# A transformer block on one core: the second visit's second stage starts two products later, and VectorE makes the low halves of both 64-row operands

## Chip, cores and metric

The kernel runs on one core of one Trainium2 chip. The metric is the device time of one execution in microseconds; the time before is a median of 3 runs.

## What is computed

One block with adaptive layer normalisation over 2048 tokens of width 576, all in fp32: attention with 32 query heads of width 18 and one shared key and value head, then an MLP of width 4608.

```python
mod = (_silu(c) @ w_mod).reshape(c.shape[0], 6, 1, -1)
sa, ca, ga, sb, cb, gb = (mod[:, i] for i in range(6))
h = _layernorm(x) * (1 + ca) + sa
x = x + ga * attention(h, wq, wk, wv, wo)
h = _layernorm(x) * (1 + cb) + sb
y = _layernorm(h)                       # the MLP normalises once more
h = _gelu(y @ w1 + b1)                  # 576 -> 4608, tanh form
x = x + gb * (h @ w2 + b2)              # 4608 -> 576
```

## The kernel before

Only the MLP, the last part of the kernel, is touched. It works on two halves of 1024 tokens. For each half it walks over 18 groups of 256 hidden columns, so there are 36 visits, `v` = 0 to 35; visit 17 is the last of the first half and visit 18 the first of the second. The loop over `v` starts at line 1208.

Each matrix product of a visit is done by a Strassen-like scheme with seven products instead of eight. In the first stage these are A11, S2, S3, A12, S1, A22 and S4, issued in that order by `product` (line 1042). To keep fp32 accuracy every operand is split into a high half, rounded to the matmul's type (a ScalarE copy), and a low half, the rest (a subtraction). Each product is 6 matmuls: high by high, high by low and low by high for two blocks of 128 rows. The width 576 is four blocks of 128 rows and one of 64. The 64-row rest is held in the tile `opt` (`TL[0]` in the code) as the operands t0 and t1, high and low half each; A12 and A22 read t0, and S1 and S4 read t1, with two further matmuls each.

`op_pieces` (line 956) holds the table of these operands: name, first block in the destination, first block in the source, and the engine that does the low-half subtraction. The function it returns, `form`, reads strings such as "+t0 -t0": plus is the high half (ScalarE, line 974), minus is the low half (line 976), and "=T1" is a sum of blocks (line 967). The engine `e2` is VectorE for what is formed before the loop and GpSimd afterwards. The operands of the second half of the tokens are formed in pieces by `more` during visits 17 and 18: "-t0" at the end of visit 17, "-t1" after product S2 of visit 18. GpSimd does there also the sum for T1, and the low halves of B21, T4 and B22.

After the first stage come the GELUs (`gelu`, line 1056), on ScalarE and VectorE. A GELU is cut into three parts; each call of `g_()` moves every open one forward by a part. The sums of GELU outputs that the second stage needs are made by GpSimd (`sums`, line 1116): `s_()` does the next of four, first S3's, then S2's, S1's and S4's. Each is one or two additions, a cast to the high half (line 1123) and a subtraction for the low half (line 1124).

The second stage of visit v (`fc2s`, line 1138) is interleaved with the first stage of visit v + 1. It is a generator with seven steps, for S3, A22, A11, A12, S2, S1 and S4, called by `t_()`. A step issues 12 matmuls into two `psA` tiles, two evictions by VectorE that add them to the residual (line 1156; line 1154 where a sum is begun), and the load of the step's weights for the next visit on the SyncE queue. S3, A11, S2 and S1 begin new `psA` tiles. There are two of these, so a step that begins new ones waits for the evictions of the step before; the other steps add to what is in the tiles, and their matmuls wait for those evictions too. In a usual visit the order on TensorE is A11, step 7 of the visit before the last, S2, step 1, S3, step 2, A12, step 3, S1, step 4, A22, step 5, S4, step 6. In visit 1 there is no seventh step of an earlier visit, so the first step comes behind A11 and S2. The four `psB` tiles hold the results of the products.

The SyncE queue also carries, behind each product, the load of that product's weights for the next visit (`w_`, line 1232). The layer normalisation of the second half of the tokens (`ln2_pair`) runs in visits 1 to 17, a piece in each call of `more`. The order of instructions on each engine is the order written in the program.

Of the kernel before, what the change touches and what calls it, by code (L numbers as in the profile page):

```python
# [32 lines left out]
def block_kernel(ctx: ExitStack, tc, x, wqkv, wo, w1, b1, w2, b2, c, wmod, ident_in, out):  # L33
    nc = tc.nc
    ve, ac, po, pe, sy = nc.vector, nc.scalar, nc.gpsimd, nc.tensor, nc.sync
# [17 lines left out]
    def psB(): return PS["t"].tile([128, 512], F32, name="psB", bufs=PS["b"])  # L53
# [650 lines left out]
    def load_w1(i, what):  # L704
        for w in what.split():
            a = 4 * OPS.index(w) if w in OPS else 28
            b = min(a + 4, 31)
            sy.dma_start(W1["r"][:, a:b].bitcast(F32), w1scr[i, :, a:b])
# [117 lines left out]
    def step(q):  # L826
        if q:
            try:
                next(q[0])
            except StopIteration:  # L830
                q.popleft()
# [124 lines left out]
    def op_pieces(R, e2):  # L956


        at = {"B11": (0, 0, ve), "B21": (2, 2, e2), "B22": (4, 7, e2), "T2": (6, 5, ve), "T1": (8, 5, ve),
              "T3": (10, 0, ve), "T4": (12, 2, e2), "t0": (0, 4, e2), "t1": (1, 9, e2)}  # L960
        less = {"T3": (5, 0, 0), "T4": (2, 5, 2), "T1": (7, 5, 5)}

        def form(what):
            for w in what.split():
                if w[0] == "=":
                    x, y, o = (R[:, i:i + 2] for i in less[w[1:]])
                    (e2 if w == "=T1" else ve).tensor_tensor(o, x, y, op=ALU.subtract)
                    continue
                a, r, e = at[w[1:]]
                n = 2 if w[1] in "BT" else 1  # L970
                o, lo = (OP, 14) if n == 2 else (TL[0], 2)
                hi, src = o[:, a:a + n], R[:, r:r + n]
                if w[0] == "+":
                    ac.activation(hi, src, AF.Copy)
                else:
                    e.tensor_tensor(o[:, lo + a:lo + a + n], src, hi.bitcast(F32), op=ALU.subtract)
        return form

    form = op_pieces(YR[0], ve)
    open_ps("3", 4)  # L980
    wop = {}

    def wo_tile(t, k0, k1):
        if t not in wop:
            p = psA() if t != 2 else None
            wop[t] = [psB()[:, :288] if t == 2 else p[:, h2, :288] for h2 in range(2)], p
        for h2 in range(2):
            wo_mm(NB - 1, t, h2, wop[t][0][h2], k0, k1)
        if k1 == KD:
            o, p = wop[t]  # L990
            if p is None:
                for h2 in range(2):
                    wo_add(NB - 1, t, h2, o[h2])
            else:
                Xv = XT[:, NT * (NB - 1) + t, :].rearrange("p (a b) -> p a b", a=2)
                ve.tensor_tensor(Xv, p[:, :, :288], Xv, op=ALU.add)
# [25 lines left out]
    def wo_end():  # L1022

        pwp.__exit__(None, None, None)
        mw = ctx.enter_context(tc.tile_pool(name="mw", bufs=1, reuse_waits="tile"))
        a = [mw.tile([128, 2, D], F32R, name="w2s", bufs=3) for _ in range(3)]
        a.append(W1["r"][:, 31:40].rearrange("p a b -> p (a b)").rearrange("p (f c) -> p f c", f=2))
        W2.extend(a[:2])
        W2S.extend(t.rearrange("p f (n c) -> p (f n) c", c=288)[:, i:i + 2] for t in a for i in (0, 2))
        GT.append(big())  # L1030
        g2 = mw.tile([128, 4, TB], F32R, name="gt2")
        GT.extend([g2[:, i] for i in range(4)] + [mw.tile([128, TB], F32R, name="gt3"), W1["r"][:, 36:40].rearrange("p a b -> p (a b)")])
        for k in range(7):
            load_w2s(0, k)
# [7 lines left out]
    def product(o, w, b, first=True, tail=None):  # L1042

        w = 4 * OPS.index(w)
        h, l = W1["r"][:, w:w + 2], W1["r"][:, w + 2:w + 4]
        terms = []
        for k in range(2):
            terms += [(h[:, k], OP[:, b + k]), (h[:, k], OP[:, 14 + b + k]), (l[:, k], OP[:, b + k])]
        if tail:
            wt = W1["r"][:, 28 + tail[0]]  # L1050
            terms += [(wt, TL[0][:, tail[1]]), (wt, TL[0][:, 2 + tail[1]])]
        for i, (x, y) in enumerate(terms):
            pe.matmul(o, x, y, start=(first and i == 0), stop=(i == len(terms) - 1), skip_group_check=True)  # L1053
# [46 lines left out]
    def pair_end():  # L1100
        v = NG - 1
        for to in ((1, 0), (1, 1), (0, 1)):
            eb_add(v, *to)
            yield
        for t in range(2 * NT):
            sy.dma_start(out[128 * t:128 * (t + 1), :], XT[:, t, :])
            yield
# [84 lines left out]
    def t_():  # L1192
        step(f2)

    def s_():
        step(sm)

    def g_():

        for gen in list(gens):  # L1200
            if next(gen, 0) == 0:
                gens.remove(gen)

    form = op_pieces(YR[0], po)
    b2_scaled(B2["b"])
    mark = [None]

    for v in range(NV):
        nxt = (v + 1) % NG
        if v == NG - 1:  # L1210
            while fill:
                step(fill)
            form = op_pieces(YR[1], po)

        def more(half="", first="", room=False):

            if v in (0, NG - 1, NG):
                form(first if v == 0 else half if v == NG - 1 else {"+T4": "-T4 +T1 -B22", "-T4": "-T1 -t1"}.get(first, ""))
            elif v > NG + 1 and fill:
                step(fill)  # L1220
            elif 0 < v < NG and fill and (room or mark[0] != "T"):
                mark[0] = next(fill[0], "end")
                if mark[0] == "end":
                    fill.popleft()
            if v == 0 and rest:
                for _ in range(2):
                    if rest:
                        wo_tile(*rest.popleft())
                if not rest:
                    wo_end()  # L1230

        def w_(w):
            if v + 1 < NV:
                load_w1(nxt, w)

        if v == NG + 1:
            fill.append(pair_end())
        ba = psB()
        product(ba, "A11", 0)
        w_("A11")  # L1240
        ac.activation(U[:, 0], ba, AF.Copy)
        g_()
        s_()
        more("+B11", "+T4")
        if v > 1:
            t_()
        bb = psB()
        product(bb, "S2", 6)
        w_("S2")
        ve.tensor_tensor(U[:, 0], bb, U[:, 0], op=ALU.add)  # L1250
        t_()
        g_()
        more("-B11 +T2", "-T4")
        bc = psB()
        product(bc, "S3", 10)
        w_("S3")
        ve.tensor_tensor(U[:, 1], bc, U[:, 0], op=ALU.add)
        s_()
        more("-T2 =T3", "+B22", True)
        t_()  # L1260
        product(ba, "A12", 2, False, (0, 0))
        w_("A12")
        gens.append(gelu(v, 0, 0, ba))
        g_()
        s_()
        more("+T3 +B21", "-B22", True)
        t_()
        g_()
        bd = psB()
        product(bd, "S1", 8, True, (1, 1))  # L1270
        w_("S1")
        be = psB()
        ve.tensor_tensor(be, bd, U[:, 1], op=ALU.add)
        g_()
        gens.append(gelu(v, 1, 1, be))
        g_()
        more("-T3 -B21")
        t_()
        g_()
        product(bc, "A22", 12, False, (1, 0))  # L1280
        w_("A22")
        ve.tensor_tensor(bc, bc, U[:, 0], op=ALU.add)
        g_()
        gens.append(gelu(v, 1, 0, bc))
        g_()
        more("=T4 +t0")
        t_()
        g_()
        product(bd, "S4", 4, False, (2, 1))
        w_("S4 tails")  # L1290
        ve.tensor_tensor(bd, bd, U[:, 0], op=ALU.add)
        g_()
        gens.append(gelu(v, 0, 1, bd))
        g_()
        t_()
        more("=T1 +T4 -t0 +B22 +t1")
        if v == NV - 1:
            while f2:
                t_()
        if v < NV - 1:  # L1300
            sm.append(sums(v))
            s_()
            f2.append(fc2s(v))
        else:
            f2.append(fc2(v))
# [44 lines left out]
```

## Time and profile before

| | |
|---|---|
| median of 3 runs | 2281.99 us (2280.32 to 2283.0) |
| the profiled execution | 2280.29 us, span 2278.5 us |
| TensorE matmul, share of the span busy | 98% (16534 instructions) |
| VectorE, ScalarE, GpSimd | 85%, 72%, 66% |
| matmuls of the first stage, blocks of 128 rows (line 1053) | 1512, 395.7 us busy |
| matmuls of the second stage with operands in the tile `big` (line 1150) | 1680, 248.3 us busy |

Times inside the execution count from the start of the span. The MLP's loop fills it from about 1410 us on. Rows of the form "line engine operation output<-input" give the line of the kernel, and the part in brackets at the end of a timeline row is how long the engine sat idle before it and which instruction ended that wait. PEld is the load of TensorE's stationary operand, which runs ahead of the matmul that uses it.

### The profile page before, as it was taken

How to read it: one execution, taken by the hardware profiler on the slowest of the kernel's cores; microseconds unless marked ns; L12 is line 12 of the kernel's file. 1: busy time of each engine (PE TensorE's matmuls, PEld its weight loads, DVE VectorE, ACT ScalarE, POOL GpSimd, SP SyncE). 2: the span in 40 equal slices, each digit the busy share in tenths (PEclk: the TensorE clock that was granted, in tenths of full speed). 3: DMA queues.
4: the chain of work that ended last, by engine and by line, in shares of the span. 5: the costliest groups of instructions: out<-in, count | busy, mean ns of one | idle time of the engine just before them, and what ended most of it. 6: DMA issues, size and time to landing. Idle time of an engine off the chain costs nothing.

```text
span 2278.5 us, 45948 instructions
## 1 busy us (share of the span) xinstructions
PE 2241.0 (98%) x16534; PEld 1446.2 (63%) x16534; DVE 1942.0 (85%) x3435; ACT 1644.9 (72%) x3141; POOL 1506.1 (66%) x1759
## 2 busy tenths in 40 slices
PE   8999999999999999999999999999999999999999
PEld 6644545444444444444444546888888878888888
DVE  6589999999999999999999974778888777787786
ACT  5558999999999999999999997444454444343443
POOL 6503366676787787677783002888888887767676
PEclk9999999999999999999999999999999999999999
DMA  6421234433433333333331002555656557666563
GB/s 225 138 99 49 73 124 142 136 128 117 135 124 121 119 132 114 119 125 123 119 129 64 20 7 83 180 174 178 177 173 180 160 151 215 180 178 179 177 181 117
DMA packets 184229, 305.58 MB, mean 134 GB/s; under 512 B 19275, under 2 KB 77515, under 8 KB 184001
## 3 DMA queue, kind: packets, MB, share of 16 engines
q1 hardware_dynamic: 184001, 302.64, 42.1%
q8 instruction: 131, 2.15, 0.4%
q14 instruction: 97, 0.79, 0.1%
HBM read 200.48 MB, written 93.19 MB: 129 GB/s over the span
## 4 chain that ended last, share of the span: by engine, by line
PE 90%; DVE 5%; POOL 2%; ACT 2%; issue 1%; DMA 0%; ACTq 0%; POOLq 0%; DVEq 0%
PE psC L845 22%; PE psB L1053 17%; PE psA L1150 16%; PE psB L855 14%; PE psM L315 11%; PE psB L657 2%; PE psB L244 2%; DVE mx L877 2%; PE psB L865 2%; PE psB L152 1%; ACT P L857 1%; PE psA L315 1%; PE psB L199 1%; PE psA L1180 1%; PE psA L657 1%
## 5 line engine op out<-in xcount | busy, mean ns | idle before, releaser
L857 ACT ACTIVATE P<-psB 128x512 f32<-128x512 f32 x2008 | 1044.8, 619 | 45.3 <-PE psM L315 18.4
L877 DVE TENSOR_REDUCE mx<-psM 128x1 f32<-128x512 f32 x1476 | 938.1, 683 | 42.4 <-PE psB L855 19.6
L315 PE MATMUL psM<-KS,qst 64*128 64x512 f32 x1722 | 600.1, 440 | 1.1 <-DVE mx L877 0.4
L855 PE MATMUL psB<-qst,KS 64*128 64x512 f32 x2008 | 584.5, 428 | 0.6 <-DVE mx L333 0.4
L845 PE MATMUL psC<-P,V 128*32 128x256 f32 (+3 forms) x6424 | 578.8, 448 | 0.5 <-ACT O L672 0.5
L855 PEld LDWEIGHTS psB<-qst,KS 64*128 64x128 f32 x2008 | 302.2, 184 | 215.6 <-ACT P L857 132.8
L1053 PE MATMUL psB<-ops,w1a 128*128 128x512 f32 x1512 | 395.7, 397 | 0.2 <-DVE h L1068 0.2
L315 PEld LDWEIGHTS psM<-KS,qst 64*128 64x128 f32 x1722 | 274.5, 184 | 157.2 <-DVE mx L877 122.4
L1053 PEld LDWEIGHTS psB<-ops,w1a 128*128 128x128 f32 x1512 | 271.4, 189 | 45.9 <-DVE h L1068 0.4
L1156 DVE TENSOR_TENSOR XT<-psA,XT 128x576 f32<-128x576 f32 x350 | 256.4, 753 | 18.5 <-PE psA L1150 11.5
L845 PEld LDWEIGHTS psC<-P,V 128*32 128x32 f32 x6424 | 139.4, 108 | 202.9 <-issue 176.7
L1150 PE MATMUL psA<-w2s,big 128*128 128x288 f32 x1680 | 248.3, 297 | 6.4 <-POOL big L1123 2.6
L1150 PEld LDWEIGHTS psA<-w2s,big 128*128 128x128 f32 x1680 | 240.0, 190 | 21.7 <-POOL big L1123 3.5
L1124 POOL TENSOR_TENSOR big<-s,big 128x512 fp32r<-128x512 f32 x140 | 181.9, 1299 | 11.2
L1066 ACT ACTIVATE psB<-gs 128x512 f32<-128x512 f32 x144 | 86.7, 602 | 135.5 <-DVE gs L1065 135.5
L1062 ACT ACTIVATE h<-psB,b1t 128x512 f32<-128x512 f32 x144 | 98.0, 680 | 109.1 <-PE psB L1053 93.7
L875 DVE CUSTOM_DVE_ANT_0 xc<-psM,xc 128x512 f32<-128x512 f32 x246 | 166.0, 681 | 3.7 <-PE psB L855 1.2
L868 ACT ACTIVATE xc<-psB 128x512 f32<-128x512 f32 x246 | 152.9, 622 | 11.9 <-PE psM L315 11.9
L691 POOL TENSOR_TENSOR os<-O,os 128x512 fp32r<-128x512 f32 x28 | 36.1, 1290 | 150.5 <-ACT os L690 150.5
L1065 DVE SCALAR_TENSOR_TENSOR gs<-psB,h 128x512 f32<-128x512 f32 x144 | 98.5, 684 | 39.3 <-ACT psB L1063 39.3
L718 POOL TENSOR_TENSOR r<-r,r 128x256 fp32r<-128x256 f32 (+1 forms) x162 | 121.4, 749 | 13.0
L132 POOL MEMSET qst<- 32x1024 f32 x62 | 58.6, 945 | 106.8 <-PE psB L855 69.0
(198 smaller groups left out, 3238.9 us busy)
## 6 DMA issues: line engine op xcount, KB each, us to landing
w1a<-w1scr SPq DMA_DIRECT2D x252, 256.0 KB
w2s<-w2sum SPq DMA_DIRECT2D x140, 288.0 KB
w1scr<-r SPq DMA_DIRECT2D x126, 256.0 KB
w2scr<-r SPq DMA_DIRECT2D x72, 288.0 KB
w2sum<-r SPq DMA_DIRECT2D x72, 288.0 KB
w2s<-w2scr SPq DMA_DIRECT2D x70, 288.0 KB
qst<-qscr SPq DMA_DIRECT2D x192, 72.0 KB
w1a<-w2scr SPq DMA_DIRECT2D x35, 288.0 KB
```

Of the source, the lines that this page charges most:

```text
L315: pe.matmul(o, QST[n][64 * g:64 * g + 64, p, 128 * qt:128 * (qt + 1)], KS[64 * g:64 * g + 64, 512 * kb:512 * (kb + 1)], start=True, stop=True)
L718: po.tensor_tensor(o[:, n:2 * n], src, o[:, :n].bitcast(F32), op=ALU.subtract)
L845: pe.matmul(PVt[n][32 * j:32 * (j + 1), cs], V[:, kc, :], t[:, j, cs], start=(kc == 0 and h0 == 0), stop=(kc == 15), skip_group_check=True)
L855: pe.matmul(t, KS[64 * g:64 * g + 64, 128 * kc:128 * (kc + 1)], QST[n][64 * g:64 * g + 64, i, :], start=True, stop=True)
L857: ac.activation(P[n, kc][:, 2 * i + g, :], t, AF.Exp, scale=SCALE)
L868: ac.activation(XC[-1], t, AF.Relu)
L875: ve.tensor_tensor_reduce(c, t, c, 1.0, -3.0e38, ALU.add, ALU.max, o)
L877: ve.tensor_reduce(o, t, axis=AX.X, op=ALU.max)
L1053: pe.matmul(o, x, y, start=(first and i == 0), stop=(i == len(terms) - 1), skip_group_check=True)
L1124: po.tensor_tensor(unit(u, 1), x, unit(u, 0).bitcast(F32), op=ALU.subtract)
L1150: pe.matmul(p[:, i, :288], x[:, ts_], W2S[k][:, y], start=(bool(first) and q == 0), stop=(q == 2), skip_group_check=True)
L1156: ve.tensor_tensor(o, p[:, :, :288], o, op=ALU.add)
```

## The change

In visit 1, and only there, the calls of `t_()` after products S2 and S3 are left out, and a second call is added after S1 and after A22. The order on TensorE in visit 1 becomes A11, S2, S3, A12, step 1, S1, steps 2 and 3, A22, steps 4 and 5, S4, step 6. And in the table of operands t0 and t1 get VectorE (`ve`) in place of `e2`. This concerns the two low halves that are formed in visits 17 and 18, since before the loop `e2` is VectorE anyway.

```diff
         at = {"B11": (0, 0, ve), "B21": (2, 2, e2), "B22": (4, 7, e2), "T2": (6, 5, ve), "T1": (8, 5, ve),
-              "T3": (10, 0, ve), "T4": (12, 2, e2), "t0": (0, 4, e2), "t1": (1, 9, e2)}
+              "T3": (10, 0, ve), "T4": (12, 2, e2), "t0": (0, 4, ve), "t1": (1, 9, ve)}
...
         product(bb, "S2", 6)
         w_("S2")
         ve.tensor_tensor(U[:, 0], bb, U[:, 0], op=ALU.add)
-        t_()
+        if v != 1:
+            t_()
         g_()
...
         more("-T2 =T3", "+B22", True)
-        t_()
+        if v != 1:
+            t_()
         product(ba, "A12", 2, False, (0, 0))
...
         more("-T3 -B21")
         t_()
+        if v == 1:
+            t_()
         g_()
         product(bc, "A22", 12, False, (1, 0))
...
         more("=T4 +t0")
         t_()
+        if v == 1:
+            t_()
         g_()
         product(bd, "S4", 4, False, (2, 1))
```

## The prediction

> **What bounds the kernel now.** I read the page first (TensorE is busy nearly throughout), then the table by stretches, then the list of waits around the two edited places, then the timelines there, engine by engine. The stretches come first. Their columns are: stretch, its length, the busy time of TensorE (PE), of its weight loads (PEld), of VectorE (DVE), ScalarE (ACT) and GpSimd (POOL), then the granted TensorE clock, the DMA share and GB/s.
>
> ```profile
> core 0: us, PE busy (x) PEld busy (x) DVE busy (x) ACT busy (x) POOL busy (x), PEclk, DMA share, GB/s
> 1427.22:1430.64 3.42, 1.39 (x6) 0.77 (x5) 2.81 (x6) 2.96 (x5) 2.73 (x3) 1.00 1.04 372
> 1430.64:1437.46 6.82, 6.13 (x19) 5.21 (x20) 2.96 (x6) 0.00 (x0) 6.44 (x8) 0.50 0.22 72
> 1850.48:1853.89 3.41, 0.43 (x3) 0.14 (x2) 0.05 (x1) 0.60 (x1) 3.41 (x4) 1.00 0.55 163
> 1853.89:1857.30 3.41, 3.41 (x14) 3.31 (x15) 2.04 (x3) 1.50 (x3) 3.19 (x4) 0.50 0.02 5
> 2256.67:2260.08 3.41, 1.98 (x15) 1.78 (x14) 3.32 (x5) 1.92 (x4) 3.41 (x4) 1.00 0.00 0
> 1480.00:1780.00 300.00, 299.29 (x1753) 265.57 (x1752) 242.95 (x382) 139.65 (x237) 252.70 (x249) 1.00 0.59 175
> ```
>
> The last row is the steady MLP: TensorE works 299.29 of 300 us at full clock. VectorE has 19% and GpSimd 16% to spare. So a microsecond of TensorE idleness removed early in the MLP should reach the end. The other rows are the exceptions. In the second visit (v = 1) TensorE is idle for 2.03 of 3.42 us and then gets half its clock for 6.82 us. Around the start of the nineteenth (v = 18, the first visit of the second row half) it is idle for 2.98 of 3.41 us and then has half the clock for 3.41 us. Idleness of 1.43 us in such a stretch (the row at 2256.67) had left the clock alone. I take the boundary to lie between 1.43 and 2.03 us.
>
> The waits of TensorE name who was late, first for the second visit, then for visit 18:
>
> ```profile
> PE psA L1150 <- POOL big L1123: 2.2, 1, 2.2
> PE psA L1150 <- POOL big L1124: 0.5, 1, 0.5
> ```
>
> ```profile
> PE psB L1053 <- POOL opt L976: 3.0, 1, 3.0
> PE psA L1150 <- POOL big L1124: 0.5, 1, 0.5
> ```
>
> In the second visit the second stage waits for GpSimd's first sum (S3's halves). In visit 18 the product S1 waits 3.0 us for the low half of t1, a 64-row operand. These are the two places that the diff edits.
>
> What lowers the clock is told differently by the Trainium skill: TensorE: Matmul & The Clock Gate (Part 1: The HAM clock gate, and HAM oscillation) says that the array falls to half rate after an idle window of about 3.4 us and advises against gaps over that. By it the 2.2 us wait would have cost no clock, and part one below would be worth 0.7 instead of 3.8 us. The stretch at 1427.22 shows a window that was idle for 2.03 us, not 3.4, and half the clock behind it: the measurement decides.
>
> **Part one: the second stage of v = 1 starts two products later.** What it removes: waits of 2.2 + 0.5 us, and the half clock, which over 6.13 busy us costs 6.13 / 2 = 3.1. Together 5.8 us. The prices of what comes instead are from TensorE's weight loads in the same visit:
>
> ```profile
> 1430.82 0.50 PEld L1150 LDWEIGHTS psA<-w2s,big 128*128 128x128 f32 x2 [2.65 <-POOL big L1123]
> ...
> 1444.08 1.74 PEld L1150 LDWEIGHTS psA<-w2s,big 128*128 128x128 f32 x12
> 1445.77 1.24 PEld L1053 LDWEIGHTS psB<-ops,w1a 128*128 128x128 f32 x6
> 1447.06 0.42 PEld L1053 LDWEIGHTS psB<-opt,w1a 128*128 128x128 f32 x2
> 1447.53 1.75 PEld L1150 LDWEIGHTS psA<-w2s,big 128*128 128x128 f32 x12
> ```
>
> One step of the second stage (12 matmuls) takes 1445.77 - 1444.08 = 1.69 us; a product of 6 takes 1.29; one with its two tail matmuls 1.76. TensorE was free for the second stage at 1430.82 - 2.65 = 1428.17. Now products S3 and A12 come there.
>
> ```profile
> 1430.85 1.27 POOL L1124 TENSOR_TENSOR big<-s,big 128x512 fp32r<-128x512 f32 x1
> ...
> 1443.95 1.30 POOL L1124 TENSOR_TENSOR big<-s,big 128x512 fp32r<-128x512 f32 x1
> ```
>
> ```profile
> 1428.06 0.69 DVE L1068 SCALAR_TENSOR_TENSOR h<-psB,h 128x512 f32<-128x512 f32 x1
> ...
> 1444.51 0.70 DVE L1273 TENSOR_TENSOR psB<-psB,u 128x512 f32<-128x512 f32 x1 [0.51 <-PE psB L1053]
> 1445.12 0.68 DVE L1068 SCALAR_TENSOR_TENSOR h<-psB,h 128x512 f32<-128x512 f32 x1
> 1445.72 1.41 DVE L1156 TENSOR_TENSOR XT<-psA,XT 128x576 f32<-128x576 f32 x2
> ```
>
> S3 needs a psB bank. By the order in which the four are released it is the one that visit 0's third GELU reads last, at 1428.06 + 0.69 = 1428.75. So S3 waits 0.6. It ends at 1430.1, A12 at 1431.85. The first step then begins; its first two matmuls use the high half, and the low half is there at 1430.85 + 1.27 = 1432.12, about when the third comes up. No wait. GpSimd's four sums keep their order and their times, as no second-stage step issues anything on it. The last, S4's, is there at 1445.25; its step comes in visit 2, at about 1450.
>
> The doubled steps are the price. After S1 two steps run in succession, and after A22 two more. Each pair shares psA: the second step may not write a bank before VectorE has read the first step's sum. In the rows at 1444.51, VectorE does the product's add and a GELU multiply before the first eviction, which at 1.41 / 2 = 0.70 ends at 1446.4, 2.34 us after the step's first load at 1444.08. TensorE would be ready for the second step at 1.69. The wait is 0.65, with the signal 0.7, and there are two pairs: 1.4 us. If the evictions come at once it is nothing; if one more GELU operation (0.68) stands ahead, it is 1.4 a pair. I take 0.7, since the order in the program is that of the rows. None of these idle times is near 2.03 us, so the clock stays up.
>
> The steps' DMAs move too. Each step issues the load of its weights for visit 2, on the queue that also loads the products' weights. The first two go out later by two products, and only the reload of S3's and A12's blocks for visit 2 comes earlier. They have a visit, over 20 us, before they are used: nothing. The loads for A12 and S1 in visit 1 are needed some 8 us sooner. The DMA share falls from 1.04 to 0.22 at 1430.64, so all that was queued has landed about then; A12's were ahead of the others in that queue. I cost it at nothing, at most 0.5.
>
> Part one: 5.8 - (0.6 + 1.4) = 3.8 us saved, between 2.4 and 5.2.
>
> **Part two: the low halves of t0 and t1 on VectorE.** The tile's instructions (count, then ns least/median/greatest) give both prices:
>
> ```profile
> L976 DVE TENSOR_TENSOR opt<-yr,opt x2: 685/1306/1928, 1407.6 to 1413.1; 128x512 fp32r<-128x512 f32 x2
> L976 POOL TENSOR_TENSOR opt<-yr,opt x2: 1274/1280/1287, 1836.4 to 1852.4; 128x512 fp32r<-128x512 f32 x2
> ```
>
> GpSimd loses two instructions of 1.28 us. VectorE gains two of 0.69 to 1.93. What stretches it is seen where both engines subtract in SBUF:
>
> ```profile
> 1825.84 1.30 POOL L1124 TENSOR_TENSOR big<-s,big 128x512 fp32r<-128x512 f32 x1
> 1825.93 2.29 DVE L976 TENSOR_TENSOR ops<-yr,ops 128x1024 fp32r<-128x1024 f32 x1
> ```
>
> VectorE starts 0.09 us behind GpSimd and takes 2.29: it waits out GpSimd's 1.30, then does its own work. So a moved subtraction first waits for whatever GpSimd is at, and then holds GpSimd's next one for 0.69. SBUF — State Buffer of the Trainium skill (section "Who interferes with whom") has the rule that speaks against this edit: of a VectorE instruction with two SBUF inputs and a GpSimd one that reads SBUF, the later is blocked wholly until the earlier ends. The trace agrees, with 2.29; without the blocking part two would be worth 4.3 us, with it 2.9.
>
> ```profile
> 1844.38 2.16 POOL L1124 TENSOR_TENSOR big<-s,big 128x512 fp32r<-128x512 f32 x1
> 1846.49 4.76 POOL L976 TENSOR_TENSOR ops<-yr,ops 128x1024 fp32r<-128x1024 f32 x2
> 1851.20 1.27 POOL L1074 TENSOR_TENSOR big<-h,big 128x512 fp32r<-128x512 f32 x1
> 1852.42 1.27 POOL L976 TENSOR_TENSOR opt<-yr,opt 128x512 fp32r<-128x512 f32 x1
> ```
>
> ```profile
> 1841.90 1.55 DVE L1156 TENSOR_TENSOR XT<-psA,XT 128x576 f32<-128x576 f32 x2 [0.81 <-PE psA L1150]
> 1843.37 0.68 DVE L1068 SCALAR_TENSOR_TENSOR h<-psB,h 128x512 f32<-128x512 f32 x1
> 1843.97 1.41 DVE L976 TENSOR_TENSOR ops<-yr,ops 128x1024 fp32r<-128x1024 f32 x1
> 1845.31 0.68 DVE L1257 TENSOR_TENSOR u<-psB,u 128x512 f32<-128x512 f32 x1
> ```
>
> ```profile
> 1847.13 1.78 PEld L1150 LDWEIGHTS psA<-w2s,gt 128*128 128x128 f32 x12
> ...
> 1856.88 0.33 PEld L1053 LDWEIGHTS psB<-ops,w1a 128*128 128x128 f32 x1
> ```
>
> Removed: the waits of 3.0 and 0.5, and half of 3.41 us at half clock, 1.7: 5.2 us.
>
> t0's subtraction, at the end of v = 17, delays VectorE by 0.7; VectorE's idle 0.81 before 1841.90 covers that, and a blocked one would cost up to 1.1 there. GpSimd gains 1.28 - 0.69 = 0.6, which ends the 0.5 wait for S3's low half. So all that follows comes 0.5 earlier.
>
> t1's subtraction stands in VectorE's queue behind that of T1, done at 1845.38. GpSimd's L1124 was held by T1's, which is why it took 2.16, and goes first, to 1846.54. Then t1's 0.69, to 1847.2. L1257 and all behind it on VectorE start 1.9 later, less the 0.5: 1.4. The first eviction of the A22 step, at 1845.31 + 0.6 + 0.7 = 1846.6 now, ends at 1848.0, and the A11 step needs that bank. TensorE is there at 1847.13 - 0.5 = 1846.6: a new wait of 1.4.
>
> The wait for t1 is gone, but next comes A12's step. Its third matmul needs the low half that GpSimd makes at 1851.20 (L1074), behind two big subtractions, done at 1852.47. It gains 1.28 from t0's leaving and loses 0.69 twice: 1852.6. TensorE gets there at 1848.0 + 1.69 + 1.76 + two matmuls of 0.14 = 1851.7: a wait of 0.9. Part two: 5.2 - (1.4 + 0.9) = 2.9 us, between -0.3 and 4.3 (the rivals).
>
> **Sum.** 3.8 + 2.9 = 6.7 us. The profiled execution took 2280.29 us with a span of 2278.5, so I expect 2273.6 of such a one; it lies 1.7 under the median of 2281.99, and from the median I get **2275.3 us**. The 1.4 us wait is close to what lowers the clock; if it does, that costs 1.7, 2277.0.
>
> **Rivals.** *The port is free.* If t1's subtraction finds GpSimd between instructions, the A11 step isn't late, L1074 ends at 1851.2, TensorE, there at 1846.6 + 1.69 + 1.76 + 0.28 = 1850.3, waits 0.9 for it, and part two is worth 5.2 - 0.9 = 4.3: 2273.9. For it: GpSimd pauses between instructions. Against it: the row of 2.16 shows one already waiting. 23%.
>
> *VectorE gets stuck behind a big subtraction.* If t1's comes up behind one of the two in the 4.76 row (2.38 each) instead of L1124, the A11 step waits 3.8, the clock halves for a stretch (1.7), and part two loses 0.3: 2278.5. 12%.
>
> *The pairs stall the array (slower).* If VectorE is two GELU operations later than in the rows, a pair's wait passes 2.03 us in one stretch and the clock halves, as now. With both pairs, at 2.03 + 3.1 each and the 0.6, visit 1 loses 10.8 instead of 5.8: 5.0 lost, 2.9 gained, 2284.1, up to 2288 with waits of 4 us. It decides from 2.03 us on; the rows give 0.7. 12%.
>
> *Visit 1's gain is given back.* If GpSimd, with the normalisation of the second row half beside its sums, can't start visit 2 sooner, only part two stays: 2279.1. Against it: the 16% that it has free. 8%.
>
> That t0 and t1 are formed elsewhere, so that the second edit does nothing, is excluded: exactly two GpSimd instructions write that tile.
>
> **Numbers.** Forecast 45%, its own range 2273.6 to 2277.0. Range 2271.5 to 2280.0: the bounds of both parts added (2.1 and 9.5 us) and all cases but the stalled pairs, with a little below for a half-clock stretch that falls otherwise. A measurement can tell about 0.2%, 4.6 us, from no change, so faster means under 2277.4: 23 + 43 of the forecast + 4 of the stuck case + 1 = 71%. Slower is half of the stalled pairs and a remainder, 7%; the rest, 22%, is no change.
>
> **What would show it.** In visit 1: no 2.2 us wait for L1123, full clock from 1427 to 1440, two short waits of the second steps of the pairs on L1156. In visit 18: no wait for the opt tile; a wait of the A11 step on L1156 and one of A12's on L1074 in its place. Clock at half near visit 1, or the A11 step late by over 2 us, would make the prediction wrong.

## The result and the profile after

The changed kernel takes a median of 2274.43 us (7 runs, 2273.23 to 2277.43) against 2280.25 us before, measured beside it (7 runs, 2279.42 to 2283.0). The ratio is 0.9975 with a 95% interval of 0.9964 to 0.9986: faster by 5.8 us, between 3.2 and 8.2, a quarter of a per cent. The forecast was 6.7 us.

The table by stretches shows the MLP's visits 1, 17 and 18 of the changed kernel. Each stretch begins with the first weight load of product A11. The first ends with that of the next visit, and the third with the first weight load of A22, behind which the two kernels run alike. The columns are those of the prediction's first fence.

```profile
core 0: us, PE busy (x) PEld busy (x) DVE busy (x) ACT busy (x) POOL busy (x), PEclk, DMA share, GB/s
1427.81:1451.04 23.23, 22.14 (x124) 19.00 (x123) 18.98 (x31) 12.10 (x21) 21.02 (x23) 1.00 0.67 209
1803.45:1833.76 30.31, 25.13 (x134) 21.54 (x135) 25.97 (x31) 13.74 (x22) 28.93 (x19) 0.94 0.48 137
1833.76:1851.88 18.12, 16.67 (x97) 14.23 (x96) 16.42 (x23) 9.15 (x15) 17.67 (x13) 1.00 0.57 155
```

The same three stretches of the kernel before took 27.25, 30.29 and 21.61 us. So visit 1 became 4.0 us shorter and visit 18 3.5, at full clock, and visit 17 in between stayed as it was. The stretches that lie between and behind these agree within 0.3 us. The profiled spans differ by less, 2278.5 - 2273.7 = 4.8 us, because the changed kernel's execution came to visit 1 2.4 us later, at 1427.81 instead of 1425.41. It lost this in parts of the program that the change does not touch. Some 1.6 us were lost near 140 us, where its clock was at half for 10.24 us; before, in the same stretch, it was at 0.83. The other 0.7 came at 580 us, where ScalarE (L690) waited 1.60 us for VectorE instead of 0.91.

```profile
133.01:136.42 3.41, 2.15 (x12) 1.16 (x11) 3.18 (x4) 0.00 (x0) 0.00 (x0) 1.00 0.47 155
136.42:146.66 10.24, 10.24 (x40) 5.22 (x38) 7.45 (x12) 6.87 (x13) 0.00 (x0) 0.50 0.75 259
```

```profile
136.42:146.66 10.24, 9.37 (x51) 4.28 (x51) 8.75 (x14) 7.88 (x15) 0.00 (x0) 0.83 0.81 283
```

(The first two rows are of the kernel after, the last of before.) What lowered the clock there is open: in the stretch ahead TensorE was idle for only 1.26 us, and in the 10.24 us at half clock it was never idle. Differences of a few microseconds are therefore read visit by visit here, not from whole spans.

In visit 1 the waits that are left are these, in the timeline of the changed kernel. The bracket is the idle time before the row and what ended it:

```profile
1431.21 2.64 PEld L1053 LDWEIGHTS psB<-ops,w1a 128*128 128x128 f32 x12 [0.64 <-DVE h L1068]
...
1434.36 1.74 PEld L1150 LDWEIGHTS psA<-w2s,big 128*128 128x128 f32 x12
...
1440.25 1.62 PEld L1150 LDWEIGHTS psA<-w2s,gt 128*128 128x128 f32 x12 [0.66 <-DVE XT L1156]
...
1446.03 1.61 PEld L1150 LDWEIGHTS psA<-w2s,big 128*128 128x128 f32 x12 [0.69 <-DVE XT L1156]
```

The first is S3 waiting for its bank, the second the first step of the second stage, with no wait for GpSimd, and the last two are the second steps of the two pairs. There is no wait for a load of weights, so the earlier loads cost nothing, as the prediction had put it.

In visit 18 two waits took the place of the 3.0 us for t1. Here are VectorE's and GpSimd's rows around t0 and t1, and the two waits of TensorE, each by its weight loads (PEld) and by its matmuls (PE):

```profile
1835.99 0.76 DVE L976 TENSOR_TENSOR opt<-yr,opt 128x512 fp32r<-128x512 f32 x1
1836.27 0.96 POOL L1123 CAST big<-s 128x512 fp32r<-128x512 f32 x1
...
1841.99 2.15 POOL L1124 TENSOR_TENSOR big<-s,big 128x512 fp32r<-128x512 f32 x1
...
1842.91 1.77 DVE L976 TENSOR_TENSOR opt<-yr,opt 128x512 fp32r<-128x512 f32 x1
...
1844.10 5.19 POOL L976 TENSOR_TENSOR ops<-yr,ops 128x1024 fp32r<-128x1024 f32 x2
...
1845.21 1.41 DVE L1156 TENSOR_TENSOR XT<-psA,XT 128x576 f32<-128x576 f32 x2
...
1846.01 1.63 PEld L1150 LDWEIGHTS psA<-w2s,gt 128*128 128x128 f32 x12 [1.26 <-DVE XT L1156]
1846.01 1.86 PE L1150 MATMUL psA<-w2s,gt 128*128 128x288 f32 x12 [0.82 <-DVE XT L1156]
...
1849.24 1.28 POOL L1074 TENSOR_TENSOR big<-h,big 128x512 fp32r<-128x512 f32 x1
...
1850.58 1.36 PEld L1150 LDWEIGHTS psA<-w2s,big 128*128 128x128 f32 x10 [0.80 <-POOL big L1074]
1850.58 1.59 PE L1150 MATMUL psA<-w2s,big 128*128 128x288 f32 x10 [0.57 <-POOL big L1074]
```

t1's subtraction took 1.77 us instead of 0.69: GpSimd was in L1124 until 1844.14. The A11 step waited for the evictions behind it, and the A12 step for L1074.

### The profile page after: what moved, and what is told of

It reads as the page before. It is cut to its first block, busy times and chain, and to the rows that moved or that the text cites. A ratio compares the mean times of both kernels' runs of the same rounds, so it can differ in the third digit from the quotient of the medians.

```text
span 2273.7 us, 45948 instructions
## 1 busy us (share of the span) xinstructions
PE 2239.4 (98%) x16534; PEld 1443.8 (63%) x16534; DVE 1944.6 (86%) x3437; ACT 1645.7 (72%) x3141; POOL 1504.5 (66%) x1757
## 4 chain that ended last, share of the span: by engine, by line
PE 88%; DVE 5%; POOL 4%; ACT 2%; issue 1%; DMA 0%; SPq 0%; POOLq 0%; ACTq 0%; DVEq 0%
PE psC L845 21%; PE psB L1053 17%; PE psA L1150 16%; PE psB L855 13%; PE psM L315 11%; PE psB L244 2%; PE psB L657 2%; DVE mx L877 2%; PE psB L865 2%; ACT P L857 1%; PE psB L152 1%; PE psA L315 1%; PE psA L1180 1%; PE psB L199 1%; PE psA L657 1%
## 5 line engine op out<-in xcount | busy, mean ns | idle before, releaser
L1156 DVE TENSOR_TENSOR XT<-psA,XT 128x576 f32<-128x576 f32 x350 | 256.1, 753 | 15.6 <-PE psA L1150 8.9
L1124 POOL TENSOR_TENSOR big<-s,big 128x512 fp32r<-128x512 f32 x140 | 182.1, 1301 | 11.2
```

Of the source, the lines that this page charges most:

```text
L1124: po.tensor_tensor(unit(u, 1), x, unit(u, 0).bitcast(F32), op=ALU.subtract)
L1156: ve.tensor_tensor(o, p[:, :, :288], o, op=ALU.add)
```

## Experiments

The theory: the gain is the sum of two independent parts. In each a wait of TensorE and, as the greater part of it in visit 1, the half clock behind that wait go away, and shorter waits on VectorE and GpSimd come instead. The rivals: one of the parts does it all; the clock has another cause; GpSimd gives the gain back later.

Visit lengths in us from the profiles (visit 18 up to A22's load):

| kernel | visit 1 | visit 17 | visit 18 | median (runs), and of before beside it |
|---|---|---|---|---|
| before | 27.25 | 30.29 | 21.61 | 2280.25 (7) |
| after | 23.23 | 30.31 | 18.12 | 2274.43 (7), 2280.25 (7) |
| first part alone | 23.30 | 30.32 | 20.29 | 2276.24 (11), 2280.16 (33) |
| second part alone | 26.44 | 30.54 | 18.13 | 2277.98 (11), 2280.16 (33) |
| wait filled | 24.88 | 30.28 | 21.71 | 2277.42 (11), 2280.16 (33) |
| one product later | 24.29 | 30.31 | 21.20 | 2277.07 (11), 2280.16 (33) |
| t1 alone | 26.41 | 30.33 | 19.03 | 2279.00 (1), 2281.17 (21) |
| t0 alone | 26.39 | 30.45 | 20.79 | 2280.99 (1), 2281.17 (21) |
| visit 17 reordered | 23.26 | 32.49 | 20.11 | 2279.68 (11), 2281.17 (21) |
| visit 17 and B22 | 23.26 | 32.47 | 21.34 | 2280.10 (11), 2281.17 (21) |
| visit 18 reordered | 23.36 | 30.32 | 16.21 | 2273.60 (6), 2280.36 (16) |
| B21 on VectorE | 23.26 | 32.52 | 17.83 | 2277.62 (11), 2280.36 (16) |
| all three | 23.26 | 29.36 | 15.97 | 2271.93 (5), 2280.36 (16) |

**The parts by themselves.** The first part alone is the changed kernel with the old engines for t0 and t1:

```diff
-              ... "t0": (0, 4, ve), "t1": (1, 9, ve)}
+              ... "t0": (0, 4, e2), "t1": (1, 9, e2)}
```

> Only the second visit's order is changed; t0's and t1's low halves stay on GpSimd. If the two parts are independent and each carries to the end: visit 1 (first weight load of A11 to that of visit 2) takes 23.2 us as in the kernel with both parts, against 27.25 before, visit 18 up to A22's load takes 21.6 as before, and the time is about 4.0 us under that of before (2276.2 beside 2280.25). If visit 1's gain is given back by GpSimd in the visits behind it: under 1 us of gain, 2279.5. If the gain of the whole change came from visit 18: no gain here.

Measured: ratio 0.9986 (0.9977 to 0.9995), 3.9 us. Visit 1 took 23.30 us, so its gain does not need the second part. Visit 18 came out at 20.29, 1.3 under the kernel before, although nothing in it had changed and t1 was still waited for 3.0 us. The stretches show why:

```profile
1844.97:1848.39 3.42, 1.99 (x10) 1.33 (x8) 1.71 (x3) 0.70 (x2) 3.42 (x3) 1.00 0.54 146
1848.39:1851.80 3.41, 1.83 (x13) 1.79 (x14) 1.30 (x3) 0.00 (x0) 3.33 (x4) 1.00 0.21 71
1851.80:1855.21 3.41, 3.41 (x22) 3.05 (x22) 2.85 (x5) 2.36 (x4) 3.19 (x4) 1.00 0.41 103
```

In these traces the clock changes only at the borders of stretches of 3.41 us. In the kernel before it fell at 1430.64 and at 1853.89, 124 x 3.413 us apart. Here the borders are others: from 1848.39 to 1853.89 it is 5.50 us, 1.6 stretches, so the stretches do not start with the program. This time the 3.0 us of idleness lay on two of them, 1.43 and 1.58, and the clock stayed up (third row). Before, one stretch held 2.98 of it and half the clock followed.

The second part alone is the kernel before with the two engine entries changed.

> Only t0's and t1's low halves go to VectorE; visit 1 is as before. If the parts are independent: visit 1 takes 27.25 us, visit 18 up to A22's load 18.1 instead of 21.6, TensorE's 3.0 us wait for the opt tile is replaced by 0.8 on L1156 and 0.6 on L1074, and the time is 3.5 us under that of before (2276.8 beside 2280.25). If the blocking by GpSimd takes the gain back: under 1 us.

Measured: ratio 0.9991 (0.9982 to 1.0), 2.2 us, with an interval that reaches no change; the timed runs alone do not show this part's gain. The profile shows visit 18 at 18.13 us, the same as with both parts, and the waits as expected. Visit 1 was 26.44 and not 27.25, again by the clock (one stretch at half instead of two). The two parts' gains, 3.9 and 2.2, add to 6.1 against 5.8 for both, but with some 2 us of doubt on each that shows little. The visits show it: 23.30 and 18.13 us with one part each, 23.23 and 18.12 with both. The parts are independent, and neither does it alone.

**What the half clock costs.** The kernel before, with matmuls that keep TensorE busy during the wait in visit 1 (their results are not used):

```diff
+        if v == 1:
+            for p in (psA(), psA()):
+                for _ in range(7):
+                    pe.matmul(p[:, 0, :128], ident, ident, start=True, stop=True)
         t_()
```

> The kernel before with 14 idle-filling matmuls (128x128 identity, results unused) behind product S2 in visit 1, in the time in which TensorE waits for S3's sum. Nothing else moves: the sum is ready at the same time. If half the clock is the price of a stretch with 2.03 us of idleness: TensorE keeps its full clock, the step still starts when the sum is there, and visit 1 takes 27.25 - 3.1 = 24.2 us, so the time is 3 us under that of before. If the clock falls only behind a whole idle stretch of 3.4 us, or for another reason, the fill changes nothing: 27.25 us and the same time, or up to 0.5 more.

```profile
1429.08 3.29 PE L1254 MATMUL psA<-ident 128*128 128x128 f32 x28
1432.12 0.51 PE L1150 MATMUL psA<-w2s,big 128*128 128x288 f32 x2
1432.81 1.58 PE L1150 MATMUL psA<-w2s,big 128*128 128x288 f32 x10 [0.18 <-POOL big L1124]
```

The second stage still waits for GpSimd's sum, yet its 10 matmuls take 1.58 us, where before they took 2.77, and visit 1 takes 24.88 us at full clock: 2.4 us less with no work moved. The fill came out longer than the first wait, but it delayed nothing, since the low half of the sum came as before: the row of 10 begins 1432.81 - 1426.04 = 6.77 us after the visit's start, and before 1432.17 - 1425.41 = 6.76. So the half clock cost 2.4 us there and not 3.1, which is why 24.2 was not reached. Timed, the ratio is 0.9989 (0.9981 to 0.9998), 2.7 us. The half clock is caused by the idleness, and it is 2.4 of the 4.0 us that the change won in visit 1.

**One product instead of two.** In visit 1 only the `t_()` behind S2 is left out, and one is doubled, behind S1.

> The second stage of visit 1 begins one product later instead of two (behind S3; one doubled step, behind S1); t0 and t1 as before. The first step's high half and low half are then waited for some 0.6 and 1.1 us, beside S3's 0.4 for its bank; one pair waits 0.5. If these stay under the boundary and the clock stays up: visit 1 takes 21.4 + 2.6 = about 24.2 us, 3 us under before, so most of the gain is from the clock and one product would nearly do. If they are over the boundary together: half the clock for a stretch or two (1.7 to 3.1 us), 25.9 to 27.3 us.

Visit 1 took 24.29 us at full clock, as the first reading has it. The second stage then waits 0.4 and 0.8 us for GpSimd. The second product of delay brings 1.1 us more (23.23).

**t0 and t1 apart.** One engine entry each in the kernel before.

> The kernel before, with only t1's low half on VectorE. If GpSimd's queue ahead of A12's low half (L1074) is what sets visit 18 once the wait for t1 is gone: S3's 0.5 us wait stays, L1074 ends about 0.4 us later than before instead of 1.0 earlier, and visit 18 up to A22's load takes 19.0 us, between 21.6 (before) and 18.1 (both). If the wait for t1 was all of it: 18.6 or less.

> The kernel before, with only t0's low half on VectorE. S3's 0.5 us wait goes, and t1's subtraction, still on GpSimd, is done some 0.9 us sooner; TensorE comes 0.5 sooner too, so its wait for t1 is 2.6 instead of 3.0. If the stretch that holds this wait is idle over the boundary the clock halves as before: 20.7 us up to A22's load; if the wait falls on two stretches: 19.4. If t0 was a side matter: 21.6.

Each was run once, so only the profiles are read. Visit 18 took 19.03 us with t1 alone and 20.79 with t0 alone (its clock halved again), both as expected of GpSimd's queue. t0's move is not a side matter: it is what lets A12's low half be ready sooner. With t1 alone it was there 17.69 us after the visit's start, with both 16.76. The t1 kernel's visit 1 shows also how narrow the clock's boundary is:

```profile
1432.11:1435.53 3.42, 1.80 (x11) 1.57 (x12) 1.91 (x5) 0.60 (x1) 3.20 (x4) 1.00 0.30 108
1435.53:1438.94 3.41, 3.41 (x12) 2.84 (x11) 2.00 (x4) 0.00 (x0) 3.26 (x4) 0.50 0.34 94
```

An idleness of 3.42 - 1.80 = 1.62 us was followed by half the clock, where 1.58 was not. It is not a sharp value, though. In visit 17 of the last kernel below (all_three) nearly the same idleness, 3.41 - 1.80 = 1.61 us, cost no clock:

```profile
1814.90:1818.31 3.41, 1.80 (x8) 1.01 (x6) 3.41 (x5) 2.25 (x3) 3.33 (x3) 1.00 0.57 158
1818.31:1821.73 3.42, 3.27 (x18) 2.73 (x18) 3.36 (x4) 2.04 (x4) 3.26 (x4) 1.00 0.12 21
```

**Visit 17.** The long wait that both kernels have in visit 17 (3.3 us on L1156) looked like an easy gain. In the changed kernel the A22 step is called ahead of the operands' pieces there:

```diff
+        if v == NG - 1:
+            t_()
         more("-T2 =T3", "+B22", True)
-        if v != 1:
+        if v not in (1, NG - 1):
             t_()
```

> The changed kernel, and in visit 17 the A22 step (matmuls and evictions) is issued ahead of T2's low half and T3's sum on VectorE instead of behind them. If these two, slowed by GpSimd, are what TensorE's 3.3 us wait on L1156 in visit 17 is: the wait goes and with it the half clock behind it (1.7), visit 17 takes about 25.8 instead of 30.3 us, and the time is 4.5 us under that of the changed kernel (2270). If the wait only moves to the evictions of the next step: it shrinks to 2 us at best, 29 us, 1 to 2 us under.

Neither reading came true: 2279.68 us, ratio to before 0.9995 (0.9986 to 1.0004), so the reordering gave back nearly all that the change had won. Visit 17 took 32.49 us. The rows at its end:

```profile
1828.51 2.27 DVE L967 TENSOR_TENSOR yr<-yr 128x1024 f32<-128x1024 f32 x1 [3.49 <-POOL ops L976]
1830.70 1.41 DVE L1156 TENSOR_TENSOR eb<-psA,eb 128x576 f32<-128x576 f32 x2
...
1831.55 3.22 PE L1150 MATMUL psA<-w2s,big 128*128 128x288 f32 x12 [5.38 <-issue]
```

VectorE's sum for T4 (L967) overwrites what GpSimd's low half of B21 (L976) must first read, and GpSimd was not there yet. The profile names no releaser for TensorE's 5.4 us, but its matmuls began as the first of the two evictions behind the sum ended (1830.70 + 0.7). Then t1 met one of the rivals of the prediction:

```profile
1843.70 2.88 DVE L976 TENSOR_TENSOR opt<-yr,opt 128x512 fp32r<-128x512 f32 x1
```

It stood behind a big GpSimd subtraction for 2.2 us, the A11 step waited 2.2 us, and the clock fell. The same kernel, with B22's low half issued behind L1074 in visit 18:

> As visit17_reordered, and in visit 18 B22's low half is issued behind the low half of A12's operand (L1074) on GpSimd instead of ahead of it. If the 2.4 us of B22 in that queue is what A12's step waits for: its 0.6 us wait goes, visit 18 up to A22's load takes 17.5 instead of 18.1 us, 2269.5. If L1074 is late for another reason (its ScalarE copy), no change, or up to 1 us more from B22 being late for S4.

It did no better: 2280.10 us, and visit 18 took 21.34 us instead of 17.5. The A11 step waited 2.9 us for evictions behind t1, so this run cannot show what B22's place does.

**Visit 18 again, and GpSimd's load.** From the changed kernel, t1's low half goes behind the A22 step's evictions and B22's behind L1074:

```diff
-   {"+T4": "-T4 +T1 -B22", "-T4": "-T1 -t1"}
+   {"+T4": "-T4 +T1", "-T4": "-T1 -B22", "-B22": "-t1"}
```

> The changed kernel; in visit 18 t1's low half comes on VectorE behind the A22 step's evictions instead of ahead of them, and B22's low half comes on GpSimd behind A12's low half (L1074). If the two waits left in visit 18 are what was read from the trace (0.8 on the evictions behind t1, 0.6 on L1074 behind B22): both go, visit 18 up to A22's load takes 16.8 instead of 18.1 us, 1.3 us under the changed kernel. If t1 now comes too late for S1, held by a big GpSimd subtraction: a wait of up to 1.5 for the opt tile in their place, no gain.

TensorE is busy for 16.16 of the 16.21 us, so no wait is left in the stretch.

```profile
1832.19:1848.40 16.21, 16.16 (x96) 14.29 (x95) 15.85 (x22) 8.37 (x13) 15.84 (x11) 1.00 0.58 161
```

Visit 18 won 1.9 us, more than the 1.3 expected. t1's subtraction did come up behind a big one of GpSimd's and took 2.21 us, but with the evictions ahead of it nobody waited. The median is 2273.60 (ratio to before 0.9968, 0.9956 to 0.998). That is 0.8 us under the changed kernel's own, which the timing cannot tell apart; the profile shows it.

Then B21's low half on VectorE too, alone and with both reorderings:

```diff
-   "B21": (2, 2, e2)
+   "B21": (2, 2, ve)
```

> The changed kernel; B21's low half too is made by VectorE (in visit 17). If GpSimd's queue is what sets visits 17 and 18, as the moved wait of visit17_reordered suggests: T4's sum no longer waits for GpSimd, GpSimd is 2.4 us freer, visit 17 is shorter by 1 to 2 us (30.3 to 29). If VectorE's evictions set visit 17: 1.2 to 2.5 us more on VectorE there, visit 17 up to 32.

> visit18_reordered, b21_on_vector and visit17_reordered together. If the 5.4 us wait that appeared with visit17_reordered was T4's sum waiting for GpSimd's B21: it goes, visit 17 takes 26 to 27 us, and the time is 4 to 5 us under the changed kernel. If VectorE sets visit 17 in any order: 30 us or more, and only the 1.3 us of visit 18.

By itself it made visit 17 longer, 32.52 us, as its second theory had it: VectorE's evictions came later. All three together take 29.36 us there and have the lowest median here: 2271.93 us, ratio to before 0.9961 (0.9948 to 0.9973). The interval overlaps that of visit 18's reordering alone, and 26 to 27 us for visit 17, or 4 to 5 us under the changed kernel, were not reached: a wait of 2.5 us on L1156 and one of 1.2 on L1074 stay.

## Why the prediction was right

*S3's bank*: 0.6 us was worked out, 0.64 measured. *The first step*: no wait, as said. *The pairs*: 0.7 each, 0.66 and 0.69 measured on the weight loads. *The clock in visit 1*: full. *Part one*: 3.8 us forecast, 4.0 in the profiles and 3.9 (1.1 to 5.2) in the timed runs of the part alone. Nothing was given back behind visit 1: visits 2 to 17 took 382.61 us before and 382.72 after. But two terms of the sum were off, and their errors nearly cancel, which is luck. The waits that went were taken from TensorE's matmuls (2.2 + 0.5), those that came from its weight loads (0.6, and twice 0.7). The old waits by the weight loads, first the second one of visit 1, then the two of visit 18:

```profile
1432.17 2.42 PEld L1150 LDWEIGHTS psA<-w2s,big 128*128 128x128 f32 x10 [0.85 <-POOL big L1124]
1434.50 2.28 PEld L1053 LDWEIGHTS psB<-ops,w1a 128*128 128x128 f32 x6
1436.88 2.02 PEld L1150 LDWEIGHTS psA<-w2s,gt 128*128 128x128 f32 x12
...
1841.07 1.36 PEld L1150 LDWEIGHTS psA<-w2s,big 128*128 128x128 f32 x10 [0.75 <-POOL big L1124]
...
1853.75 0.19 PEld L1053 LDWEIGHTS psB<-opt,w1a 128*128 128x128 f32 x1 [3.41 <-POOL opt L976]
```

In this measure 2.65 + 0.85 = 3.50 us of waits went in visit 1, 0.8 more than was put, and 0.64 + 0.66 + 0.69 = 1.99 came. Of the 4.02 us that leaves 2.5 for the clock, 0.6 less than was put, and near the 2.4 of the filled wait. Work at half clock did not take twice as long: a product of 6 took 1436.88 - 1434.50 = 2.38 us where it takes 1.29 at full clock, 1.8 times.

*Part two*: 2.9 us forecast, 3.5 in the profiles, with the same two terms off. By the weight loads 0.75 + 3.41 = 4.16 us of waits went, where 3.5 was put, and 1.26 + 0.80 = 2.06 came, where 1.4 + 0.9 = 2.3 was put. Of the 3.49 us that leaves 1.4 for the clock, where 1.7 was put; the first part alone, whose clock stayed up, gives 21.61 - 20.29 = 1.3. So the two new waits were named and sized well, and t1's stay behind L1124 was as worked out (1.8 us against the 1.77 row). One price behind them was too high: 0.69 us of GpSimd's time for each of VectorE's two subtractions. The rows of the result show 0.96 - 0.61 = 0.35 for the cast behind t0 and 5.19 - 4.76 = 0.43 for the pair behind t1. GpSimd's instruction began when the subtraction had only 0.48 and 0.58 us left, by the same rows.

*The sum*: 6.7 us from one profile, 5.8 timed, and 6.7 lies well inside the interval of 3.2 to 8.2, so the 0.9 us between them need no cause. What the sum rests on least firmly is the clock's loss of one execution, used for all. Visit 1 took 27.25 us in the profile before and 26.4 in the three other profiles in which it was as before. Visit 18 took 21.61 there, and 20.29, 21.20 and 21.71 in three others. Over these four profiles each, the mean gain against the changed kernel is 3.4 and 3.1 us, together 6.5.

*The rivals*: the free port did not come; the stalled pairs did not, at 0.7 us each; the gain was not given back. t1 stuck behind a big subtraction did not come in the changed kernel either, but in visit17_reordered it did, with the wait and the clock that the rival named.

## What to carry to other kernels

A wait of the matmul engine has two prices, its length and the clock behind it, and the second can be as large as the first (2.4 us beside 2.7 in visit 1). Here several short waits were cheaper than one long one, and even useless matmuls in the gap paid. Take the waits that go and those that come from the same kind of rows: a wait here was 0.2 to 0.5 us longer by the weight loads than by the matmuls. When a wait is removed in a program whose engines hold each other up and overwrite each other's operands, list what is queued behind each moved instruction on its new engine: a reordering that looked better from TensorE's side alone lost nearly as much as the whole change had won. Microseconds in milliseconds are read per stage from the profile: visit 1 of the seven kernels with the changed order took 23.23 to 23.36 us, while the runs of one kernel lay 3 to 7 us apart.

## What the runs showed of the hardware

In the MLP the clock halved after a stretch of 3.41 us with 1.62 us of idleness and not after ones with 1.58 and 1.61, so the boundary lies near 1.6 us, less than half a stretch. Near the start of the program the rows do not fit it: the clock halved after 1.26 us of idleness (the row at 133.01), and in b21_on_vector it stayed up after 3.41 - 1.78 = 1.63 (47.67 to 51.08). A single wait of 3.0 us cost no clock when it fell on two stretches, and 1.3 us when it fell on one; which it is changes from execution to execution. At half clock a product of 6 took 2.38 us instead of 1.29, 1.8 times. VectorE's subtraction in SBUF of 0.69 us took 0.76, 1.77, 2.21 or 2.88 us by what GpSimd was doing, and held GpSimd's next instruction by 0.35 to 0.43.
